# Attention and two MoE layers on one core: each score computed once instead of twice, with its exponential transposed

## The chip, the cores and the metric

The kernel runs on one core of a Trainium2 chip. A core has TensorE (PE in the profile; PEld is its weight load), VectorE (DVE), ScalarE (ACT), GpSimd (POOL) and SyncE (SP), which issues most of the DMAs. Each takes its instructions in order, and they meet through semaphores. SBUF holds 128 partitions by columns; TensorE writes to PSUM, here 8 banks of 128 x 512 fp32. The metric is the device time of one execution in microseconds (us).

## The reference

```python
# attention: q, k, v are (2, 8, 1152, 64)
q_pool = q.reshape(B, H, S // 2, 2, D).mean(axis=3)
scores = scale * np.matmul(q_pool, k.transpose(0, 1, 3, 2))
scores = scores - np.max(scores, axis=-1, keepdims=True)
attn = np.exp(scores)
attn = attn / (np.sum(attn, axis=-1, keepdims=True) + 1e-09)
out = np.matmul(attn, v)
x = out.transpose(0, 2, 1, 3).reshape(1152, 512)
# MoE 1: (1152 x 512) @ (512 x 2048), a rational function of h, @ (2048 x 512)
# MoE 2: the same shapes, with softplus between the products
```

Two queries are averaged into one, so each of the 16 heads has 576 query rows against 1152 keys of 64 columns.

## The kernel before, in words

Heads are taken in pairs: 8 pairs, then MoE 1, then MoE 2. Every fp32 operand of a product is split into a rounded part and the remainder (`fp32r`, names ending in h and l, or hi and lo), and a product is built from two or three passes of such parts. A pair's queries and keys are loaded, transposed on TensorE (`tr_k`, `tr_q`), split by ScalarE (the rounded part) and VectorE (the remainder), and brought by SBUF-to-SBUF DMAs into `KS`, `QQ` and `QL` (`ksXy`, `qqXy` and `qlXy`: X is the pair's parity, y the head).

The attention computes each score twice. `p1_fill` (L431) computes it with queries on partitions, 128 rows by 384 keys, only for the row maximum, which VectorE takes (`p1_max`, L437). There are 27 such units in a pair: 9 row tiles of 128 queries over both heads, times 3 blocks of keys. The maxima are transposed and written as extra rows beside the query remainder (`shift_a`, `shift_t`, `shift_m`). `s_step` (L482, L483) computes the score again with keys on partitions, 128 x 288, and these extra rows subtract the maximum within the product. ScalarE takes the exponential (L489) and rounds two of them together to `ph` (L500); GpSimd subtracts to `pl`; `pv` multiplies in three passes (L516 to L518), the denominator as 64 columns of -1 beside V. In the last pair PV is one pass over unrounded exponentials (L514). `xev_a` and `xev_b` normalise and split the result into `xh` and `xl`.

The order is written by step numbers: a pair has 36 steps, `at(t, fn)` puts work at a step, and a scheduler then orders the engines. The maxima of pair j+1 are taken in the steps of pair j. The weights of the MoE layers come as 64-bit words and are converted on the chip: `w_abs` (ScalarE), two passes of `w_conv` (VectorE), then `w_split` (ScalarE, then VectorE). Sixteen weight tiles are prepared during the attention, three of them spread over the middle pairs and thirteen at steps of four from step 15 of pair 6 on. The MoE stages stand in program order behind it. The VectorE subtractions are all in a helper, so they have its line (L126).

Of the kernel before, what the change touches and what calls it, by code (L numbers as in the profile page):

```python
# [19 lines left out]
    wu=1,  # L20
    ft=2,
    lv=0,
    pv=15,
    pvd=8,
    pe=8,
    ped=3,
    pq=8,
    tk=12,
    tkd=3,
    tke=1,  # L30
    tq=21,
    tqd=3,
    tqe=0,
    ks0=21,
    q0=27,
    ks1=35,
    q1=45,
    kh0=-17,
    kh1=2,
    p1o=-2,  # L40
    p1m=1,
    s0=23,
    s1=40,
    st0=8,
    st1=8,
    sm=0,
    sg=1,
    po=7,
    ps=9,
    xa=16,  # L50
    xb=19,
    w0=-12,
    wd=3,
    wc=14,
    wg=4,
    wh=1,
    ce=10,
    ph=1,
    xl=1,
    vl=1,  # L60
# [23 lines left out]
)


def attn_moe_kernel(tc, q, k, v, w1_in, w1_out, moe_a, moe_b, w2_in, w2_out, out):
# [21 lines left out]
    def at(t, fn, pr=0):
        ev.append((t, pr, len(ev), fn))  # L110

    def behind(fn, *engines):
        with ExitStack() as es:
            for e in engines:
                es.enter_context(tc.issue_after(st["last", e]))
            fn()

    def high(fn, *a):
        with tc.high_priority():
            fn(*a)  # L120
# [858 lines left out]
```

## Time and profile before

| | |
|---|---|
| median of 3 runs (lowest, highest) | 743.1 us (742.61, 743.12) |
| profiled execution: span | 740.7 us |
| its granted TensorE clock, mean | 0.993 |
| busy: PE, DVE, ACT, POOL | 719.3, 543.4, 491.0, 228.9 us |
| score for the maximum, first | 9.2 us |
| first MoE product | 325.28 us |
| DMA | 70.76 MB, mean 96 GB/s |

The profiled execution gives its span, from the first to the last instruction, and no other time of its own; the timed runs lie 2.4 us above it. A matmul row's time is from its start to the end of its drain, so rows of consecutive matmuls overlap; the chain of waits gives the time from one to the next. Rows of ScalarE and VectorE overlap a little too.

### The profile page before, as it was taken

The numbers are of one execution on the slowest core, as the hardware profiler recorded it, in microseconds if no ns is written. First come the engines' busy times: TensorE is split into PE (matmuls) and PEld (weight loads), VectorE is DVE, ScalarE is ACT, GpSimd is POOL, SyncE is SP. The second block draws the span as 40 slices with busy tenths as digits, with TensorE's granted clock in tenths as the row PEclk, the third lists the DMA queues.
The fourth block names the chain that finished last, engine by engine and source line by source line (L and its number), as shares of the span: only waits on it lengthen the run. The fifth ranks groups of instructions, "written<-read, shape, count | busy, mean of one in ns | idle before, by whom it ended". The sixth has DMA issues, their size and how long they took to land.

```text
span 740.7 us, 11685 instructions
## 1 busy us (share of the span) xinstructions
PE 719.3 (97%) x4216; PEld 677.0 (91%) x4216; DVE 543.4 (73%) x938; ACT 491.0 (66%) x945; POOL 228.9 (31%) x197
## 2 busy tenths in 40 slices
PE   8999999999999997997999999999999999999998
PEld 5699999999999997887999999999898999999896
DVE  6877778787877679779999999999786676621122
ACT  3278888888888887877778777876465464422221
POOL 5278787878787776020000000000000000000000
PEclk9999999999999999998999999999999999999999
DMA  5776574747453434542221121210023333201011
GB/s 138 165 183 139 125 180 96 179 98 179 99 122 71 95 86 124 178 151 66 71 58 58 58 85 58 87 58 29 28 86 119 109 114 114 86 1 42 1 43 42
DMA packets 64841, 70.76 MB, mean 96 GB/s; under 512 B 24632, under 2 KB 53136, under 8 KB 64784
## 3 DMA queue, kind: packets, MB, share of 16 engines
q1 hardware_dynamic: 63600, 69.04, 35.1%
q10 hardware_dynamic: 1184, 0.98, 0.4%
q8 instruction: 33, 0.54, 0.3%
q14 instruction: 24, 0.20, 0.1%
HBM read 47.71 MB, written 2.36 MB: 68 GB/s over the span
## 4 chain that ended last, share of the span: by engine, by line
PE 81%; DVE 10%; ACT 4%; issue 3%; DMA 1%; POOL 0%; DVEq 0%; ACTq 0%; SPq 0%
PE acc L769 14%; PE h L747 13%; PE p L431 10%; PE h L666 9%; PE acc L715 9%; PE s L482 5%; PE s L483 5%; PE pv L518 4%; PE pv L516 4%; PE pv L517 4%; PE pv L514 3%; PE wm L269 1%; DMA wraw<-in_moe_w_in_dram 1%; DVE p L689 1%; DVE m L691 1%
## 5 line engine op out<-in xcount | busy, mean ns | idle before, releaser
L126 POOL TENSOR_TENSOR pl<-p,ph 128x576 fp32r<-128x576 f32 x126 | 180.9, 1447 | 53.5 <-ACT ph L500 40.8
L437 DVE TENSOR_REDUCE nm<-p 128x1 f32<-128x384 f32 x216 | 116.2, 553 | 47.8 <-PE p L431 45.6
L489 ACT ACTIVATE p<-s 128x288 f32<-128x288 f32 x252 | 100.8, 407 | 28.2 <-PE s L483 26.7
L126 DVE TENSOR_TENSOR gl<-p,gh 128x384 fp32r<-128x384 f32 (+1 forms) x72 | 49.6, 689 | 90.7 <-ACT gh L756 89.8
L666 PE MATMUL h<-xh,w 128*128 128x384 f32 x384 | 100.7, 342 | 4.4 <-DVE p L690 4.4
L747 PE MATMUL h<-xh,w 128*128 128x384 f32 x384 | 98.1, 336 | 0.1
L755 ACT ACTIVATE p<-h 128x384 f32<-128x384 f32 x48 | 23.6, 491 | 108.4 <-PE h L747 108.4
L715 PE MATMUL acc<-gh,w 128*128 128x384 f32 x384 | 92.9, 337 | 1.3 <-ACT gh L676 1.2
L769 PE MATMUL acc<-w,gh 128*128 128x512 f32 x288 | 90.1, 394 | 0.0
L500 ACT CAST ph<-p 128x576 fp32r<-128x576 f32 x126 | 84.6, 671 | 2.3
L518 PE MATMUL pv<-pl,v 128*128 128x288 f32 x252 | 74.8, 297 | 1.1 <-POOL pl L126 1.1
L666 PEld LDWEIGHTS h<-xh,w 128*128 128x128 f32 x384 | 71.2, 192 | 4.8 <-issue 4.7
L516 PE MATMUL pv<-ph,v 128*128 128x288 f32 x252 | 75.2, 299 | 0.0
L517 PE MATMUL pv<-ph,v 128*64 128x288 f32 x252 | 74.3, 295 | 0.0
L747 PEld LDWEIGHTS h<-xh,w 128*128 128x128 f32 x384 | 70.1, 188 | 4.2 <-ACT p L755 0.4
L715 PEld LDWEIGHTS acc<-gh,w 128*128 128x128 f32 x384 | 68.6, 188 | 2.8 <-ACT gh L676 2.8
L666 PE MATMUL h<-xl,w 128*128 128x384 f32 x192 | 65.4, 341 | 0.0
L747 PE MATMUL h<-xl,w 128*128 128x384 f32 x192 | 64.6, 337 | 0.0
L769 PEld LDWEIGHTS acc<-w,gh 128*128 128x128 f32 x288 | 53.5, 188 | 9.0
L715 PE MATMUL acc<-gl,w 128*128 128x384 f32 x192 | 59.3, 337 | 0.3 <-DVE gl L126 0.3
L769 PE MATMUL acc<-w,gl 128*128 128x512 f32 x144 | 56.9, 395 | 0.0
L518 PEld LDWEIGHTS pv<-pl,v 128*128 128x128 f32 x252 | 47.5, 188 | 1.9 <-POOL pl L126 1.6
(167 smaller groups left out, 1638.7 us busy)
## 6 DMA issues: line engine op xcount, KB each, us to landing
wraw<-in_moe_w_in_dram SPq DMA_DIRECT2D x32, 512.0 KB, 4.0
wraw<-in_moe_w_out_dram SPq DMA_DIRECT2D x32, 512.0 KB, 3.3
kr<-in_k_dram SPq DMA_DIRECT2D x15, 288.0 KB, 3.8
vr<-in_v_dram SPq DMA_DIRECT2D x7, 576.0 KB, 3.7
qr<-in_q_dram SPq DMA_DIRECT2D x15, 256.0 KB, 4.3
out_dram<-m SPq DMA_DIRECT2D x15, 128.0 KB, 1.8
kha<-ks0a SPq DMA_DIRECT2D x4, 288.0 KB, 3.0
khb<-ks0b SPq DMA_DIRECT2D x4, 288.0 KB
```

What stands on the lines that cost most here:

```text
L126: return eng.tensor_tensor(out=o, in0=a, in1=b, op=ALU.subtract)
L431: m = nc.tensor.matmul(out=o, lhsT=l, rhs=r, start=(a == 0), stop=(a == len(mm) - 1))
L437: nc.vector.tensor_reduce(out=st["nm", j][:, t, e:e + 1], in_=st.pop(("p1", j, u)), axis=AX.X, op=ALU.max, negate=True)
L489: st["last", "exp"] = nc.scalar.activation(out=st["p"][:, s % 2], in_=t, func=AF.Exp).ins
L500: nc.scalar.copy(out=ph, in_=p)
L516: nc.tensor.matmul(out=st["pv", j, g], lhsT=h, rhs=ph, start=(c == 0), stop=False)
L517: nc.tensor.matmul(out=st["pv", j, g][0:64], lhsT=l, rhs=ph, start=False, stop=False)
L518: nc.tensor.matmul(out=st["pv", j, g], lhsT=h, rhs=pl, start=False, stop=(c == C - 1))
L666: nc.tensor.matmul(out=h, lhsT=w[:, wi, wd], rhs=x[:, d, xcols(c)], start=(n == 0), stop=(n == 3 * ND - 1))
L715: nc.tensor.matmul(out=st["acc", c, d], lhsT=w[:, wi, wd], rhs=g, start=(first and n == 0), stop=(last and n == 2))
L747: nc.tensor.matmul(out=h, lhsT=w[:, wi, d * 128:(d + 1) * 128], rhs=x[:, d, xcols(c)], start=(n == 0), stop=(n == len(mm) - 1))
L769: nc.tensor.matmul(out=st["acc", c, t], lhsT=g[:, t * 128:(t + 1) * 128], rhs=w[:, wi], start=(first and n == 0), stop=(last and n == 2))
```

## The change

Each score is computed once, with queries on partitions, in the 128 x 384 units that before served only the maximum (`score`, L459). The three units of a row tile stay in PSUM (four buffers, pool `pS`) until VectorE has taken their maxima (L466) and the smallest of the three negated maxima (L470); ScalarE then takes the exponential in place of the second score, with that column as its bias, and has the instruction add up its row as well (L479). TensorE transposes the exponential in three 128 x 128 pieces (`spread`, L430). For two units of three ScalarE rounds the transposed tile to `ph` and VectorE subtracts to `pl`; for the third ScalarE copies it to SBUF (`c`), and GpSimd rounds and subtracts. PV takes two passes (L559): `ph` times V's both parts side by side, 128 columns, and `pl` times the rounded part. GpSimd adds the three row sums, VectorE takes the reciprocal, TensorE transposes it (64 rows), and VectorE multiplies. In all pairs, the last too, this is done alike. The copies of the keys to `KH` and the extra rows go.

The order is no longer by steps and a scheduler. Every operation gets a time: the number of its row tile (9 in a pair) plus an offset from the tables `O`, `OT` and `OJ`. `run` sorts each engine by these and emits them so. The thirteen weight tiles are put 0.8 row tiles apart, from just ahead of the last pair. One line of a table stands here for the three.

```diff
-    pp1 = sb(name="pp1", bufs=3, space=PSUM)
-    pps = sb(name="pps", bufs=3, space=PSUM)
-    ppv = sb(name="ppv", bufs=2, space=PSUM)
+    pS = sb(name="pS", bufs=4, space=PSUM)
+    pT = sb(name="pT", bufs=3, space=PSUM)
+    pA = sb(name="pA", bufs=1, space=PSUM)
...
-        nc.tensor.matmul(out=t, lhsT=KS[i][x][:, ks], rhs=QQ[i][x][:, cs], start=True, stop=False)
-        nc.tensor.matmul(out=t, lhsT=KH[x][:, ks], rhs=QL[i][x][:, cs], start=False, stop=True)
...
-        st["last", "exp"] = nc.scalar.activation(out=st["p"][:, s % 2], in_=t, func=AF.Exp).ins
...
-        nc.scalar.copy(out=ph, in_=p)
-        sub(nc.gpsimd, pl, p, ph)
...
-        nc.tensor.matmul(out=st["pv", j, g], lhsT=h, rhs=ph, start=(c == 0), stop=False)
-        nc.tensor.matmul(out=st["pv", j, g][0:64], lhsT=l, rhs=ph, start=False, stop=False)
-        nc.tensor.matmul(out=st["pv", j, g], lhsT=h, rhs=pl, start=False, stop=(c == C - 1))
...
+        b = st["t"]
+        when = b + O.get(kind, 0)
+        if kind in OT:
...
+    def run():
+        need = [set(o[3]) for o in ops]
...
+        queue = {}
+        for i in sorted(range(len(ops)), key=lambda i: (ops[i][0], i)):
+            queue.setdefault(ops[i][1], []).append(i)
+        done = [False] * len(ops)
+        with tc.manual_schedule():
+            while any(queue.values()):
+                heads = [q[0] for q in queue.values() if q and all(done[d] for d in need[q[0]])]
+                i = min(heads, key=lambda i: (ops[i][0], i))
+                queue[ops[i][1]].pop(0)
+                done[i] = True
+                ops[i][2]()
...
+MODES = "ABA"
+NS, NT_, NP_, NPH, NCP = 4, 3, 6, 5, 2
...
+        op("S" + str(e), "PE", fn=fn, R=R, W=[k], new=[("s", NS)], **mm(173 * (3 if diag else 2 * len(srcs))))
...
+        op("M" + str(n % 3), "DVE", fn=lambda: nc.vector.tensor_reduce(
+            out=NM[i][:, n:n + 1], in_=tl[k], axis=AX.X, op=ALU.max, negate=True),
+           R=[k], W=[("NM", i, n)], **dve(384))
+        if n % 3 == 2:
+            op("B", "DVE", fn=lambda: nc.vector.tensor_reduce(
+                out=MB[i][:, t:t + 1], in_=NM[i][:, 3 * t:3 * t + 3], axis=AX.X, op=ALU.min),
+               R=[("NM", i, 3 * t + e) for e in G3], W=[("MB", i, t)], **dve(3))
...
+            o = tl[p] = late.tile([128, 384], F32, tag="p", name="p", bufs=NP_)
+            nc.scalar.activation(out=o, in_=tl[k], func=AF.Exp, bias=MB[i][:, t:t + 1], accum_out=DEN[i][:, n:n + 1])
...
+        op("T" + str(e), "PE", fn=lambda: transpose(k, [(tl[p][:, a * 128:(a + 1) * 128], 128) for a in G3]),
+           R=[p], W=[k], new=[("t", NT_)], **mm(327))
...
+        if md == "A":
+            for m, (s0, w, o, h, l) in enumerate(d):
+                    act_copy(view(h, o, w), src(k, s0, w))
+                op("L" + str(e), "DVE", fn=lambda s0=s0, w=w, o=o, h=h, l=l: sub(
+                    nc.vector, view(l, o, w), src(k, s0, w), view(h, o, w)), R=[k, h], W=[l], **dve(3 * w))
...
+        def fn():
+            tl[c] = late.tile([128, 384], F32, tag="c", name="c", bufs=NCP)
+            (nc.scalar.copy if md == "B" else nc.vector.tensor_copy)(out=tl[c], in_=tl[k][:, 0:384])
...
+                nc.gpsimd.tensor_copy(out=view(h, o, w), in_=src(c, s0, w))
...
+            op("L" + str(e), "POOL", fn=lambda s0=s0, w=w, o=o, h=h, l=l: sub(
+                nc.gpsimd, view(l, o, w), src(c, s0, w), view(h, o, w)), R=[c, h], W=[l], **pool(3 * w))
...
+                mm_ = [(acc, v2[:, c], tl[h]), (acc[0:64], v2[:, c, 0:64], tl[l])]
+                for a, (o, p, r) in enumerate(mm_ if c < C - 1 else mm_[::-1]):
+                    nc.tensor.matmul(out=o, lhsT=p, rhs=r[:, m, 0:w], start=(c == a == 0), stop=(c == C - 1 and a == 1))
...
+            nc.gpsimd.tensor_add(out=r, in0=d[:, :, 0], in1=d[:, :, 1])
+            nc.gpsimd.tensor_add(out=r, in0=r, in1=d[:, :, 2])
+            nc.gpsimd.tensor_scalar(out=r, in0=r, scalar1=1e-9, scalar2=None, op0=ALU.add)
...
+        op("D1", "DVE", fn=lambda: nc.vector.reciprocal(out=r, in_=r), R=W, W=W, **dve(24))
...
+            rt, [(RC[i][:, t:t + 1].to_broadcast([128, 64]), 128) for t in GT[g]], 64),
...
+            nc.scalar.copy(out=tl[u][:, 0:w], in_=tl[k][64:128, 0:w])
...
+        op("U1", "DVE", fn=lambda: nc.vector.tensor_add(out=tl[u][:, 0:w], in0=tl[k][0:64, 0:w], in1=tl[u][:, 0:w]),
...
+            nc.vector.tensor_mul(out=tl[xs][64 * x:64 * x + 64, c0:c0 + w], in0=tl[rt][0:64, o0:o0 + w],
+                                 in1=tl[u][:, 0:w])
...
+        for h, key in enumerate((st["khi", j], st["klo", j])):
+            op(f"dk{x}", fn=lambda h=h, key=key: fdma(KS[i][x][64 * h:64 * h + 64], tl[key][r]),
+               R=[(*key, g) for g in G3], W=[("KS", i, x, h, g) for g in G3], **spq(lat=4500))
...
+        op("wl", fn=lambda: w_load(i), W=[raw], new=[("raw", 2)], **spq(lat=4000))
+        op("w0", "ACT", fn=lambda: w_abs(i), R=[raw], W=[pk], new=[("pk", 3)], **act(512))
+        op("w1", "DVE", fn=lambda: w_conv(i, 0), R=[pk], W=[pk], port=True, ns=340, lat=150)
+        op("w2", "DVE", fn=lambda: w_conv(i, 2), R=[raw, pk], W=[pk], port=True, **dve(512))
+
...
+        op("w3", "ACT", fn=fh, R=[pk] + pool_[1], W=[w], **act(512))
+        op("w4", "DVE", fn=fl, R=[pk, w], W=[w], port=True, **dve(512))
...
+        for n in range(NRA + NRB - 1):
+            a = n < NRA
+            at(te + T["ce"] + T["prea"] + n * T["pred"], weight, NE + n,
+               ((lambda: st["wra"]) if a else (lambda: st["wrb"]), [("wra",) if a else ("wrb",)]))
...
+    "S0": -1.2121,
...
```

TensorE in the middle of a pair, before (`p1` is a score for the maximum, `s` the second score, `pv` the result):

```order
L482 MATMUL s_2894<-qq0a_101,ks0a_95 128x288
L483 MATMUL s_2894<-ql0a_105,kha_99 128x288
L431 MATMUL p1_2907<-ks1a_97,qq1a_103 128x384
L431 MATMUL p1_2907<-ks1a_97,ql1a_107 128x384
L516 MATMUL pv_2879<-ph_2839,v20_111 128x288
L517 MATMUL pv_2879<-ph_2839,v20_111 64x288
L518 MATMUL pv_2879<-pl_2840,v20_111 128x288
```

A round of one score for the maximum, one PV step and one second score repeats.

The same engine now, about row tile 6 of a pair (`s` the score, `t` a transposed tile, `p` an exponential, `pv` the result):

```order
L459 MATMUL s_3979<-ks0b_101,qq0b_105 128x384
L459 MATMUL s_3979<-ks0b_101,ql0b_109 128x384
L430 MATMUL t_3982<-ident_58,p_3977 128x128 x3
L459 MATMUL s_3988<-ks0b_101,qq0b_105 128x384
L459 MATMUL s_3988<-ks0b_101,ql0b_109 128x384
L430 MATMUL t_3991<-ident_58,p_3986 128x128 x3
L430 MATMUL t_4005<-ident_58,p_3995 128x128 x3
L459 MATMUL s_4009<-ks0b_101,qq0b_105 128x384
L459 MATMUL s_4009<-ks0b_101,ql0b_109 128x384
L559 MATMUL pv_4015<-ph_3872,v20_114 128x320
L559 MATMUL pv_4015<-pl_3873,v20_114 64x320
```

Between two scores stand transposes of exponentials and pieces of PV; a score needs a buffer that an exponential of an earlier row tile has given up.

VectorE in the last pair, before (`pk` and `w` are a weight being converted, `xm`, `pv` and `xs` the normalising):

```order
L528 SCALAR_TENSOR_TENSOR xm_4802<-pv_4717,xr_4801 64x288
L186 TENSOR_SCALAR pk_4808<-pk_4808 128x512
L529 TENSOR_TENSOR pv_4717<-pv_4717,xr_4801 64x288
L192 SCALAR_TENSOR_TENSOR pk_4808<-wraw_4769,pk_4808 128x512
L532 SCALAR_TENSOR_TENSOR xs0_4653<-xm_4802,pv_4717 64x288
L126 TENSOR_TENSOR w_4817<-pk_4771,w_4817 128x512
L126 TENSOR_TENSOR w_4840<-pk_4808,w_4840 128x512
L186 TENSOR_SCALAR pk_4877<-pk_4877 128x512
```

Only weights and the normalising are left there, since the maxima of this pair were taken in the pair before.

VectorE in the last pair now (`nm` a maximum, `mb` the smallest of three, `pl` a remainder, `u` and `xs` the normalising):

```order
L313 TENSOR_TENSOR pl_4331<-t_4304,ph_4330 128x3x128
L377 SCALAR_TENSOR_TENSOR pk_4328<-wraw_4258,pk_4328 128x512
L313 TENSOR_TENSOR pl_4357<-t_4335,ph_4356 128x3x128
L466 TENSOR_REDUCE nm1_61<-s_4353 128x1
L466 TENSOR_REDUCE nm1_61<-s_4383 128x1
L466 TENSOR_REDUCE nm1_61<-s_4376 128x1
L313 TENSOR_TENSOR pl_4331<-t_4379,ph_4330 128x3x128
L470 TENSOR_REDUCE mb1_65<-nm1_61 128x1
L371 TENSOR_SCALAR pk_4395<-pk_4395 128x512
L377 SCALAR_TENSOR_TENSOR pk_4395<-wraw_4313,pk_4395 128x512
L592 TENSOR_TENSOR u_4406<-pv_4319,u_4406 64x256
L313 TENSOR_TENSOR pl_4357<-t_4412,ph_4356 128x3x128
```

The conversion of the weights now stands among the maxima, with the maxima queued behind it.

## Rows read from the trace of the kernel before

**Rows 1.** Page: the span, and the chain that ended last, by engine.

```profile
span 740.7 us, 11685 instructions
...
PE 81%; DVE 10%; ACT 4%; issue 3%; DMA 1%; POOL 0%; DVEq 0%; ACTq 0%; SPq 0%
```

**Rows 2.** Windows: one middle pair, and the last pair; busy us by engine.

```profile
133.00:170.00 37.00, 36.36 (x255) 35.71 (x254) 28.91 (x58) 32.46 (x74) 30.62 (x25) 1.00 0.59 138
293.00:332.00 39.00, 35.81 (x186) 30.95 (x185) 30.73 (x56) 28.91 (x68) 6.86 (x9) 0.96 0.55 165
```

**Rows 3.** Chain of waits, middle of a pair: start, us, TensorE line, count.

```profile
150.97 0.35 PE p L431 x2
...
151.33 0.13 PE pv L516
...
155.78 0.33 PE tk L350 x3
```

**Rows 4.** Milestones: V rows two pairs apart (chain), first score (tile), first MoE product (timeline).

```profile
117.01 1.58 DVE v L126
...
191.03 1.58 DVE v L126
...
L431 PE MATMUL p<-ks0a,qq0a x51: 335/340/446, 9.2 to 234.1; 128*128 128x384 f32 x51
...
325.28 0.72 PE L666 MATMUL h<-xh,w 128*128 128x384 f32 x2
```

**Rows 5.** ScalarE, groups by shape, and one timeline row of two exponentials.

```profile
L489 ACT ACTIVATE p<-s 128x288 f32<-128x288 f32 x252 | 100.8, 407 | 28.2 <-PE s L483 26.7
...
L356 ACT CAST khi<-tk 128x384 fp32r<-128x384 f32 x21 | 9.8, 468 | 9.3 <-PE tk L350 8.1 <-DVE nm L437 1.1
...
L526 ACT ACTIVATE xr<-pv,eps 64x288 f32<-64x288 f32 x32 | 15.9, 498 | 2.6 <-PE pv L518 1.7 <-PE pv L514 0.2
...
L259 ACT ACTIVATE b_sb<-b_sb 128x2 f32<-128x2 f32 x1 | 0.2, 202 | 0.0
...
153.92 0.70 ACT L489 ACTIVATE p<-s 128x288 f32<-128x288 f32 x2
```

**Rows 6.** VectorE: a subtraction by shape; timeline of two maxima and one weight.

```profile
L126 DVE TENSOR_TENSOR klo<-tk,khi 128x384 fp32r<-128x384 f32 x21 | 11.7, 556 | 2.2 <-ACT khi L356 1.8
...
156.12 1.02 DVE L437 TENSOR_REDUCE nm<-p 128x1 f32<-128x384 f32 x2
...
304.01 0.43 DVE L186 TENSOR_SCALAR pk<-pk 128x512 int32<-128x512 int32 x1
...
304.47 0.69 DVE L192 SCALAR_TENSOR_TENSOR pk<-wraw,pk 128x512 int32<-128x512 int32 x1
...
305.08 0.68 DVE L126 TENSOR_TENSOR w<-pk,w 128x512 fp32r<-128x512 f32 x1
```

**Rows 7.** GpSimd, groups by shape: subtraction, query sums, two kinds of copies.

```profile
L126 POOL TENSOR_TENSOR pl<-p,ph 128x576 fp32r<-128x576 f32 x126 | 180.9, 1447 | 53.5 <-ACT ph L500 40.8 <-PE pv L518 4.1 <-PE s L483 3.5
...
L339 POOL TENSOR_TENSOR qs<-qr 128x256 f32<-128x256 f32 x14 | 10.6, 773 | 10.0 <-PE tq L375 6.4 <-DMA qr<-in_q_dram 3.7
...
L540 POOL CAST xh<-xs 128x288 fp32r<-128x288 f32 x2 | 1.9, 941 | 22.1 <-DVE xs L532 22.1
...
L297 POOL CAST qq0a<-qq0a 64x512 fp32r<-64x512 f32 x1 | 0.6, 604 | 1.6 <-ACT qq0a L291 1.6
```

**Rows 8.** VectorE lines: a short reduction and a short copy, ns min/median/max.

```profile
L445 DVE TENSOR_REDUCE m<-nm x16: 151/157/173, 27.8 to 291.1; 128x5 f32<-128x15 f32 x16
...
L446 DVE CAST s<-m x16: 159/267/1874, 29.0 to 292.9; 128x5 fp32r<-128x5 f32 x16
```

**Rows 9.** TensorE timeline after its longest wait in the attention.

```profile
296.76 1.30 PE L514 MATMUL pv<-ph,p 128*128 128x288 f32 x2 [3.19 <-issue]
...
298.34 0.44 PE L516 MATMUL pv<-ph,v 128*128 128x288 f32 x1
```

**Rows 10.** DMA issues: a key copy between SBUF tiles, us to landing.

```profile
ks1a<-klo SPq DMA_DIRECT2D x4, 288.0 KB, 4.7
```

More of the change, by code (lines that the diff above doesn't have):

```diff
@@ L19 @@
     warm=24,
[L20 to L60, printed above, removed]
+    xp=1,
+    vp=1,
+    fq=-5,
+    f1=0.62,
+    fd=0.3,
+    v0=-4.2,
+    one=4,
+    ce=-1.5,
+    cv=2.5,
+    pre0=6,
+    prea=0.3,
+    pred=0.8,
     l1=2,
@@ L100, in attn_moe_kernel @@
     NCH = NT // TOK
-    ST = 4 * C
+    ST = 27
     NE, NRA, NRB = T["ne"], 7, 7
     LAG1, LAG2 = T["l1"], T["l2"]
-    ev = []
     st = {}
[L109 to L120, printed above, removed]
+    ops, wrote, read, rings = [], {}, {}, {}
@@ new lines, in attn_moe_kernel, with act, dve, pool @@
+    G3 = range(3)
+    def act(n, extra=0):
+        return dict(ns=n * 0.917 + 50 + extra, lat=150)
+    def dve(n):
+        return dict(ns=n / 0.96 + 70, lat=150)
+    def pool(n, two=True):
+        return dict(ns=n * (2.36 if two else 1.1) + 90, lat=80, port=True)
+    def mm(n):
+        return dict(ns=n, lat=240)
+    def spq(eng="SP", ns=450, lat=3500):
+        return dict(eng=eng, ns=ns, lat=lat)
+    def act_copy(out, in_):
+        nc.scalar.copy(out=out, in_=in_)
+    def transpose(k, srcs, rows=128, w=128):
+        o = tl[k] = pT.tile([128, 512], F32, tag="t", name="t")
+        for i, (a, n) in enumerate(srcs):
+            nc.tensor.transpose(o[0:rows, i * 128:i * 128 + n], a, ident[0:n, 0:n])
@@ L264, in warm @@
-    def warm(n):
-        if "wm" not in st:
-            st["wm"] = ppv.tile([128, 512], F32, tag="wm", name="wm")
-        t = st["wm"]
-        for _ in range(n):
-            nc.tensor.matmul(out=t[0:64, 0:256], lhsT=zero[:, 0:64], rhs=zero, start=True, stop=True)
-    def first_k(x, g):
-        kr = st["kr", 0]
-        t = pps.tile([128, 512], F32, tag="s", name="tk")[0:64, 0:384]
-        for i in range(3):
-            nc.tensor.transpose(t[:, i * 128:(i + 1) * 128], kr[:, x, 3 * g + i], ident)
-        s = slice(384 * g, 384 * (g + 1))
-        st["last", "act"] = nc.scalar.copy(out=KS[0][x][0:64, s], in_=t).ins
-        st["last", "dve"] = sub(nc.vector, KS[0][x][64:128, s], t, KS[0][x][0:64, s]).ins
@@ L797, in attn_moe_kernel @@
     if True:
[L798 to L815 removed]
+        attention()
+        run()
+        pA.release()
+        pT.release()
+        pS.release()
         late.release()
@@ L918, in attn_moe_kernel @@
                 if every(n, T["r2"]):
-                    behind(w_step, "gh")
+                    with tc.issue_after(st["last", "gh"]):
+                        w_step()
             m = n - 2 * LAG2
```

987 lines of the change are left out of this document (585 added, 402 removed), and 35 rows, old and new, of the table OT.

## The prediction

> **What bounds the kernel now.** I read the page first. The chain that ended last is TensorE for 81% of a span of 740.7 us, so what is worth something is what TensorE waits for or is spared [rows 1]. Next the windows: in a middle pair TensorE is busy for 36.36 of 37.00 us, ScalarE for 32.46, GpSimd for 30.62, VectorE for 28.91, at a granted clock of 1.00 [rows 2]. The attention is TensorE's work from end to end, with the others close behind. The milestones divide the span: the first score starts at 9.2 us, MoE 1 at 325.28, and between two V rows that are two pairs apart lie 74.02 us, so a pair takes 37.0 [rows 4]. MoE's code is unchanged and begins in both kernels with sixteen weights prepared or nearly so; its first 384 tokens need only pairs 0 to 3. So I take the 415.4 us from 325.28 to the end as they are and ask only when MoE 1 begins. The timed runs are 2.4 us above the span, and I carry that over.
>
> **TensorE per pair.** The chain gives the time from one matmul to the next: 0.35 us for two of 384 columns, about 0.135 for one of 288, 0.33 for three transposes [rows 3]. Before: 57 score matmuls for the maxima (24 units by two, the three of the mixed row tile by three) x 0.175 = 10.0; 72 of the second score and 108 of PV x 0.135 = 24.3; 14 transposes x 0.11 = 1.5. That is 35.8, and 1.2 us of waiting make the 37.0.
> The change takes away the 72 second scores (9.7) and one PV pass of three (4.9). It adds 81 transposes of exponentials (8.9) and 10 of reciprocals (1.1). After: scores 10.0, PV in two passes 72 x 0.135 = 9.7, transposes 105 x 0.11 = 11.6: 31.2 us. So TensorE is spared 4.6 us a pair.
>
> **The others per pair.** ScalarE: an exponential of 288 columns takes 407 ns alone and two take 0.70 us, so about 0.11 overlaps; a copy of 384 out of PSUM takes 468, hence 0.36 from start to start; a column as bias adds 91 (498 against 407, same columns) [rows 5]. No row shows the row sum taken with an exponential: its lower bound is nothing, its upper one the smallest ScalarE instruction, 202 ns [rows 5]. The two are near, and I take 0.10. 27 exponentials x 0.55 = 14.9, 27 copies x 0.36 = 9.7, four copies of the accumulator x 0.3 and five of keys and queries together 2.8: 27.4 us, or 24.7 to 30.1.
> VectorE: two maxima take 1.02 us, one 0.55, hence 0.47 a maximum and, at the like 556 ns, a subtraction [rows 6]. 27 maxima 12.7, 18 remainders 8.5, nine short reductions x 0.16 = 1.4 [rows 8], eight operations on the accumulator 3.0, keys and queries 2.2, reciprocals 0.6: 28.4 us.
> GpSimd: a subtraction of 576 columns takes 1447 ns, hence 0.96 for 384 [rows 7]. Its rounding copy has two prices: 604 ns for 512 columns, or 0.5 for 384, and 941 for 288, or 1.25. I take the former, the nearer in width, and keep the latter for the range. Nine copies 4.5 and nine subtractions 8.7, query sums 2.0, V 4.3, the output split 2.2, row sums 1.2: 22.9, or 34.4 by the dear copy. So per pair nothing is above TensorE's 31.2 but GpSimd in its bad case.
>
> **What is late next.** Before, an exponential passed from TensorE to ScalarE, to GpSimd, and back to TensorE. Now a tile crosses eight times: score, maximum, exponential, transpose, rounding, remainder, PV, normalising, and every engine works to a fixed order. I put TensorE's waits at twice the 1.2 us of before, so 33.5 us a pair; 31.2 with almost none is the lower end.
>
> **The last pair.** VectorE has no keys and queries there (26.2), but thirteen weights: from one row to the next 0.46 and 0.61, and 0.61 for the third at the same overlap [rows 6], 1.68 each, 21.8 in all. Sum 48. Before, the maxima of this pair were behind it when most weights came, and VectorE was busy for only 30.73 of 39.00 us [rows 2]. A copy between SBUF tiles that meets GpSimd takes up to 1874 ns instead of 159, while a reduction of the same size class never leaves 151 to 173 [rows 8]; the 39 weight operations are of the exposed sort. I add 3 us for blocking and take off 2 for weight work that follows the last maximum: 49 us. No blocking gives 46, 0.2 us on each operation 54.
> [...]
>
> **The sum.** First score 9.2 (loads and first transposes are as before); first exponential 2.5 later (three scores 1.05, the last one's drain, maximum, smaller reduction); seven pairs 7 x 33.5 = 234.5; the last pair 49; from its last exponential over transposing to the first MoE product 3, for MoE's first products stand ahead of the last PV group in TensorE's order. 298.2 us against 325.3: MoE begins 27.1 us earlier. 743.1 - 27.1 = 716.0 us. Break-even is a middle pair of 37.4 us.
>
> **Rivals.**
> *Almost no waits.* ScalarE and VectorE have 3 to 4 us to spare per pair and TensorE fills up: 31.6 a pair, 47 for the last. MoE begins at 282.9: 701 us. For it: the order was laid so that independent work stands between dependent steps. Against: eight crossings.
> *Keys late at the turn of a pair.* The keys of the next pair are transposed about two thirds through a pair, then split, then copied by DMA; a copy lands 4.7 us after issue [rows 10], and scores can't begin without it. From the transposes to the next pair's first score TensorE has about 7.3 us of other work, the path needs about 0.25 + 1.0 + 1.2 + 4.7 = 7.2. If it is 1.2 late each time, seven turns cost 8: 724 us. Before, keys were a whole pair ahead.
> *GpSimd bounds.* At 34.4 of work and 2 of hand-off a pair takes 36.4, and MoE begins at 318.5: 736 us. For it: both dear copies of the trace. Against: they ran in the last pair beside VectorE's weight passes, which the middle pairs hardly have.
> *The score buffers (slower).* Three of four PSUM buffers hold one row tile till its maximum is known. The loop: second exponential done, the third score of the next tile runs 0.35 and drains 0.17, maximum 0.55, reduction 0.16, two exponentials 1.2, four hand-offs 0.25: 2.7 us. With one transposed tile and a PV piece ahead on TensorE (0.9), a remainder on VectorE (0.47) and a copy on ScalarE (0.36) it is 4.4 a row tile, 39.6 a pair. The last pair is then 51: MoE begins at 342.9, 761 us. It decides from 37.4 / 9 = 4.15 on. For it: the order shows such work between scores. Against: the average row tile has 31.2 / 9 = 3.5 of TensorE's work, and the offsets spread the interposed pieces over three scores.
> [...]
> [...]
> That the second score doesn't really go is out: the order has no 288-column score left.
>
> **Chances.** The forecast 0.45; almost no waits 0.14; keys late 0.14; GpSimd 0.11; score buffers 0.08; clock 0.08. Less than 0.2% (1.5 us) can't be told from no change here. Only GpSimd's case reaches to that: 0.02 of it. Faster 0.82, same 0.02, slower 0.16. The range from 699 to 740 us takes in the first four cases and leaves out the two slower ones and the far ends.
>
> **What would show it.** Right: a pair of 32 to 35 us between V's or another pair-wise row; no score row of 288 columns, 648 rows of transposed exponentials (81 a pair); MoE's first product between 285 and 315 us and the rest 415 us long; the last pair longer than the others, VectorE over 90% busy there. Wrong: exponentials over 0.7 us, GpSimd copies over 1 us, TensorE waiting for `ks` copies at each turn, waits for ScalarE ahead of every third score, a granted clock under 0.95 in the middle, or a MoE stage that changes its length, which I have put at nothing.

## The result and the profile after

The changed kernel takes 726.1 us (median of 4 runs, 724.6 to 727.1) against 742.9: a ratio of 0.977, 95% interval 0.976 to 0.979. It is 16.8 us faster; 27.1 were forecast, and the time lies in the range but 10.1 us above the number.

The page of the changed kernel: its span, and the chain that ended last by engine. It answers to [rows 1].

```profile
span 722.7 us, 11854 instructions
...
PE 60%; DVE 19%; ACT 12%; issue 4%; DMA 2%; SPq 1%; POOL 0%; DVEq 0%; ACTq 0%
```

TensorE's share of the chain falls from 81% to 60%, and VectorE's rises from 10% to 19%: the chain now changes engine more often. Where it does so is read from milestones. The score products of three pairs, by the key tile that they read (ns of one, min/median/max, then first and last start; the first row is that of the whole span), and below them the first MoE product in TensorE's timeline; they answer to [rows 4]:

```profile
L459 PE MATMUL s<-ks0a,qq0a x51: 338/421/688, 10.3 to 237.0; 128*128 128x384 f32 x51
...
L459 PE MATMUL s<-ks1a,qq1a x12: 337/378/440, 50.2 to 64.8; 128*128 128x384 f32 x12
...
L459 PE MATMUL s<-ks0a,qq0a x12: 338/383/442, 85.3 to 99.0; 128*128 128x384 f32 x12
...
L459 PE MATMUL s<-ks1a,qq1a x12: 331/421/447, 257.4 to 274.0; 128*128 128x384 f32 x12
```

```profile
304.54 0.60 PE L970 MATMUL h<-xh,w 128*128 128x384 f32 x2
```

From first score to first score, pair 0 takes 39.9 us (10.3 to 50.2), pair 1 35.1 (to 85.3), pairs 1 to 6 together 207.2 (50.2 to 257.4, or 34.5 each), and pair 7 47.1 to the first MoE product. The MoE stage begins at 304.5 instead of 325.28, 20.8 us earlier, and 2.8 of these are lost again behind it (418.2 us to the end instead of 415.4). Busy time by engine in pair 2 and in pair 7 (length, PE, PEld, DVE, ACT, POOL, granted clock, DMA share, GB/s), against [rows 2]:

```profile
85.30:119.80 34.50, 33.08 (x235) 29.88 (x235) 30.79 (x77) 31.22 (x96) 24.48 (x44) 1.00 0.54 131
257.40:304.50 47.10, 37.34 (x244) 30.97 (x243) 46.46 (x108) 43.67 (x121) 23.36 (x37) 1.00 0.44 134
```

In a middle pair TensorE is busy for 33.1 of 34.5 us, ScalarE for 31.2, VectorE for 30.8: three engines within 2.3 us of each other. In pair 7 VectorE is busy for 46.5 of 47.1 us and ScalarE, with the same weights, for 43.7. GpSimd stands far behind (24.5 and 23.4 us). All that TensorE waited for in pair 2 (us in total, times, longest):

```profile
PE s L459 <- ACT p L479: 0.8, 2, 0.6
PE t L430 <- ACT c L529: 0.3, 1, 0.3
PE t L430 <- DVE pl L313: 0.2, 1, 0.2
```

No key copy is among TensorE's waits, and no wait ahead of every third score. The chain of waits of pairs 2 and 3 by line (85 to 154 us), and that of pair 7 (257.4 to 304.5 us); both lists go on to the right:

```profile
by line: PE t L430 23.1%; PE s L459 23.0%; PE pv L559 20.0%; ACT p L479 10.6%; ACT ph L425 5.3%; ACT u L589 3.6%; ACT c L529 3.5%; issue 3.0%; DVE pl L313 2.6%; ACT khi L699 2.4%; DVE nm L466 1.6%; ACT w L870 1.4%; DVE mb L470 0.2%; ACTq L5
```

```profile
by line: ACT p L479 16.2%; DVE nm L466 14.1%; issue 9.5%; ACT ph L425 6.9%; DVE pk L377 6.7%; DVE pk L371 5.9%; ACT pk L365 5.9%; PE t L430 5.6%; DVE pl L313 5.3%; DVE w L313 5.2%; PE s L459 4.9%; DVE xs L601 2.6%; ACT w L870 2.5%; PE pv L5
```

In the middle pairs TensorE has 66% of the chain and ScalarE 27%; in pair 7 the listed lines of VectorE sum to 40%, ScalarE's to 32%. ScalarE's timeline in pair 2 shows what the exponential with its sum costs; it answers to [rows 5]:

```profile
103.65 0.48 ACT L529 COPY c<-t 128x384 f32<-128x384 f32 x1
104.03 0.48 ACT L425 CAST ph<-t 128x384 fp32r<-128x384 f32 x1
104.43 0.58 ACT L479 ACTIVATE p<-s,mb 128x384 f32<-128x384 f32 x1
104.91 0.19 ACT L479 ACTIVATION_READ_ACCUMULATOR p<-s,mb 128x1 f32 x1
105.00 0.57 ACT L479 ACTIVATE p<-s,mb 128x384 f32<-128x384 f32 x1
105.46 0.20 ACT L479 ACTIVATION_READ_ACCUMULATOR p<-s,mb 128x1 f32 x1
105.56 0.58 ACT L479 ACTIVATE p<-s,mb 128x384 f32<-128x384 f32 x1
```

The sum is an instruction of its own with 0.2 us on its row. Adding the two durations would give 0.78 us, but they overlap: from start to start it is 0.56 to 0.57. A copy takes 0.48 on its row and 0.38 from start to start.

Where the forecast and the trace part, in us:

| Stretch | forecast | measured | off by |
|---|---|---|---|
| first score | 9.2 | 10.3 | +1.1 |
| pair 0 | 33.5 | 39.9 | +6.4 |
| pairs 1 to 6 | 201.0 | 207.2 | +6.2 |
| pair 7, to the first MoE product | 54.5 | 47.1 | -7.4 |
| MoE stage | 415.4 | 418.2 | +2.8 |
| around the span | 2.4 | 3.4 | +1.0 |

The sum is +10.1 us. The last row is no stage of the kernel: every execution lies 1.9 to 2.1 us above its own span, and the profiled one was the fastest of the four.

### The profile page after: what moved, and what is told of

Same layout as the page of the kernel before. It is cut to its first block, busy times and chain, and to the rows that moved or that the text cites. A ratio compares the mean times of both kernels' runs of the same rounds, so it can differ in the third digit from the quotient of the medians.

```text
span 722.7 us, 11854 instructions
## 1 busy us (share of the span) xinstructions
PE 685.3 (95%) x4076; PEld 629.0 (87%) x4076; DVE 559.4 (77%) x1080; ACT 495.2 (69%) x1135; POOL 205.2 (28%) x357
## 4 chain that ended last, share of the span: by engine, by line
PE 60%; DVE 19%; ACT 12%; issue 4%; DMA 2%; SPq 1%; POOL 0%; DVEq 0%; ACTq 0%
PE acc L1073 14%; PE h L1051 13%; PE s L459 8%; PE t L430 8%; PE pv L559 7%; PE acc L1019 5%; PE h L970 4%; ACT p L479 4%; DVE nm L466 2%; ACT ph L425 2%; DMA wraw<-in_moe_w_in_dram 2%; DVE m L995 2%; DVE p L993 2%; DVE m L1005 2%; DVE pl L313 2%
## 5 line engine op out<-in xcount | busy, mean ns | idle before, releaser
L466 DVE TENSOR_REDUCE nm<-s 128x1 f32<-128x384 f32 x216 | 116.5, 550 | 23.4 <-PE s L459 22.1
L479 ACT ACTIVATE p<-s,mb 128x384 f32<-128x384 f32 x216 | 125.9, 593 | 5.1 <-DVE mb L470 4.6
L430 PE MATMUL t<-ident,p 128*128 128x128 f32 x648 | 99.0, 276 | 8.8 <-ACT p L479 4.2
L1059 ACT ACTIVATE p<-h 128x384 f32<-128x384 f32 x48 | 23.6, 492 | 108.5 <-PE h L1051 108.5
L430 PEld LDWEIGHTS t<-ident,p 128*128 128x128 f32 x648 | 79.0, 142 | 18.2 <-ACT p L479 9.6
L559 PE MATMUL pv<-ph,v 128*128 128x256 f32 (+1 forms) x288 | 89.5, 321 | 1.2 <-DVE u L592 0.6
L313 DVE TENSOR_TENSOR pl<-t,ph 128x384 fp32r<-128x384 f32 (+1 forms) x160 | 80.3, 509 | 7.0 <-ACT ph L425 5.4
L425 ACT CAST ph<-t 128x384 fp32r<-128x384 f32 (+1 forms) x160 | 70.0, 453 | 18.8 <-PE t L430 12.7
L559 PE MATMUL pv<-pl,v 128*64 128x256 f32 (+1 forms) x288 | 77.4, 295 | 1.6 <-POOL pl L313 1.6
L313 POOL TENSOR_TENSOR pl<-c,ph 128x384 fp32r<-128x384 f32 (+1 forms) x80 | 75.0, 941 | 4.6
L539 POOL CAST ph<-c 128x384 fp32r<-128x384 f32 (+1 forms) x80 | 41.3, 520 | 71.6 <-ACT c L529 66.8
```

The costliest lines, as they stand in the source:

```text
L313: return eng.tensor_tensor(out=o, in0=a, in1=b, op=ALU.subtract)
L425: nc.scalar.copy(out=out, in_=in_)
L430: nc.tensor.transpose(o[0:rows, i * 128:i * 128 + n], a, ident[0:n, 0:n])
L466: op("M" + str(n % 3), "DVE", fn=lambda: nc.vector.tensor_reduce(out=NM[i][:, n:n + 1], in_=tl[k], axis=AX.X, op=ALU.max, negate=True), R= ...
L479: nc.scalar.activation(out=o, in_=tl[k], func=AF.Exp, bias=MB[i][:, t:t + 1], accum_out=DEN[i][:, n:n + 1])
L539: nc.gpsimd.tensor_copy(out=view(h, o, w), in_=src(c, s0, w))
```

## The experiments

Each is an edit of the changed kernel. Three theories stood at the start. *TensorE* sets the middle pairs, as forecast. *ScalarE* sets them instead, since a score buffer is held until the sum is read out (in pair 2 the two scores that wait for an exponential start at 105.15 and 108.98 us, each 0.05 us after the end of a sum's row). And *VectorE* alone sets pair 7, with ScalarE's nearly equal busy time as the rival.

### 1. Without the row sums

```diff
-nc.scalar.activation(..., bias=MB[i][:, t:t + 1], accum_out=DEN[i][:, n:n + 1])
+nc.scalar.activation(..., bias=MB[i][:, t:t + 1])     # DEN is set once, on GpSimd
```

> Leaves out the row sums: the exponentials are written without an accumulated sum, and the denominators are set once to a constant. In the changed kernel a middle pair takes 34.5 us, TensorE is busy for 32.0 to 32.7 of 33 to 34 us and waits 1.3 us; ScalarE is busy for 29.2 to 30.7. ScalarE's exponential with its sum takes 0.57 us to the next instruction, a copy of the same size 0.38. Theory TensorE (its work sets the middle pairs): at most its waits go, middle pair 33.2 to 34.4, pair 7 unchanged within 1 us, time 717 to 726. Rival ScalarE (each score buffer is held until the sum is read out): 27 x 0.17 = 4.6 us less in each of eight pairs, middle pair about 30, time 686 to 694.

Measured: 723.2 us (ratio 0.974, 0.972 to 0.975). Pair 2:

```profile
87.00:121.50 34.50, 33.20 (x237) 29.97 (x236) 31.01 (x78) 29.23 (x69) 24.71 (x44) 1.00 0.57 132
```

ScalarE is spared 2.0 us and the pair is as long as it was, where the rival wanted 4.6 us less. ScalarE doesn't set it. The 2.9 us that the run gains lie elsewhere: pairs 1 to 6 together take 204.5 us instead of 207.2 (1.4 of this in pair 1) and the MoE stage 416.7 instead of 418.2, while pair 0 is 3.0 longer, at a granted clock of 0.74 instead of 0.83 from 10 to 30 us. Without the sum, exponentials follow each other after 0.46 to 0.47 us, so the sum costs 0.10, as the prediction had taken it; the 0.17 of this expectation came from comparing with a copy, and was wrong.

### 2. Without the low pass of PV

```diff
-for a, (o, p, r) in enumerate(mm_ if c < C - 1 else mm_[::-1]):   # high, low
+for o, p, r in mm_[:1]:                                            # high alone
```

> Leaves out the second pass of PV, the one with the low parts of the exponentials (36 products a pair, about 0.117 us apart, 4.2 us); the low parts are still made. Theory TensorE: a middle pair goes from 34.5 to 30.9 to 32, where ScalarE (busy 30 to 31) takes over; seven pairs give 18 to 25 us, pair 7, which VectorE bounds, gives nothing; time 701 to 708. Rival ScalarE: middle pair 34 to 34.5, time 723 to 726.

Measured: 712.3 us (0.960, 0.958 to 0.962). Neither theory gave this. Pair 2:

```profile
83.90:117.10 33.20, 30.94 (x200) 25.27 (x199) 30.32 (x77) 31.29 (x95) 24.76 (x43) 1.00 0.59 139
```

TensorE lost 36 products, 4.8 us by the prediction's 0.135, and the middle pair only 1.3. ScalarE is busy for 31.3 of 33.2 us there, and in the chain of waits from 84 to 150 us its exponentials alone have 24.5%, TensorE's products and transposes together 17%, where they had 66% before this edit:

```profile
by line: ACT p L479 24.5%; ACT ph L425 9.3%; PE s L459 8.2%; ACT c L529 7.4%; issue 6.6%; PE t L430 6.4%; DMA vr<-in_v_dram 6.2%; DVE nm L466 6.2%; DVE pl L313 4.4%; ACT u L589 4.2%; ACT khi L699 3.7%; PE pv L559 2.1%; SPq L638 2.0%; SPq L6
```

So TensorE set the pair, but ScalarE stands 1.3 us behind it. Pairs 1 to 6 together are 9.8 us shorter, 1.6 each.

### 3 to 5. The thirteen weights of the last pair

Run 3 leaves out VectorE's part of them, run 4 ScalarE's, run 5 both. What is left out is replaced by fills on GpSimd:

```diff
 # run 3
-w_conv(i, 0)
-w_conv(i, 2)
-sub(nc.vector, w[:, 1], g, w[:, 0])
+nc.gpsimd.memset(w[:, 1], 0.0)
 # run 4
-w_abs(i)
+nc.gpsimd.memset(st["pk", i], 0.0)
-nc.scalar.copy(out=w[:, 0], in_=g)
+nc.gpsimd.memset(w[:, 0], 0.02)
 # run 5: both
```

> Leaves out VectorE's part of the thirteen weights that are converted in the last pair (two bit steps and the low part, 13 x 1.78 = 23 us; GpSimd clears the low part in its place). Theory VectorE bounds the last pair (99% busy there): pair 7 goes from 47.1 to the 34 to 36 of the others, time 713 to 716. Rival ScalarE bounds it just as much (it is busy 46 of 47 us there, 16 of them with the same weights): pair 7 stays at 44 to 47, time 722 to 726.

> Leaves out ScalarE's part of the same thirteen weights (the magnitude and the high part, 13 x 1.25 = 16 us; GpSimd sets both tiles instead). Theory VectorE alone bounds the last pair: pair 7 stays at 45 to 47 us, time 724 to 727. Rival ScalarE: pair 7 goes to 35 to 40, time 714 to 720. If both bound it equally, neither this kernel nor the one without VectorE's part gains more than 3 us.

> Leaves out both parts of the thirteen weights of the last pair, VectorE's (23 us) and ScalarE's (16 us); GpSimd sets the tiles. Without VectorE's part alone pair 7 went from 47.1 to 44.1 us with ScalarE busy for 43.3 of them. Theory two engines (ScalarE's work stands right behind VectorE's): pair 7 falls to 34 to 37 us, the length that TensorE sets elsewhere, and the first gate tile of the MoE stage comes 20.5 to 21.5 us after the stage's first product, as in the kernel before, instead of 23.5; time 712 to 716. Rival (the transfers of the weights, or the end of a pair itself, hold the last pair): pair 7 stays at 40 to 44, time 718 to 721.

Measured: run 3 719.5 us (0.969, 0.967 to 0.970), run 4 727.5 (0.980, 0.978 to 0.981), run 5 719.2 (0.969, 0.967 to 0.970); pair 7 takes 44.1, 51.2 and 41.8 us. Pair 7 of run 3, then of run 5:

```profile
257.00:301.10 44.10, 36.67 (x248) 31.47 (x246) 29.24 (x73) 43.33 (x121) 23.89 (x48) 1.00 0.48 152
```

```profile
257.40:299.20 41.80, 37.08 (x246) 32.78 (x245) 29.29 (x74) 32.95 (x99) 32.89 (x68) 0.96 0.58 174
```

With 17 us of work off VectorE, ScalarE is busy for 43.3 of 44.1 us: two engines bound pair 7, not VectorE alone. The time of run 3 lies below the rival's 722 to 726 because its MoE stage is 415.3 us long again. Run 4 is longer than the changed kernel, which no theory said. The first bit step of a weight, ns min/median/max, in pair 7 of the changed kernel and of run 4:

```profile
L371 DVE TENSOR_SCALAR pk<-pk x13: 407/415/960, 257.3 to 304.3; 128x512 int32<-128x512 int32 x13
```

```profile
L371 DVE TENSOR_SCALAR pk<-pk x12: 407/418/2033, 256.7 to 305.4; 128x512 int32<-128x512 int32 x12
```

The median stays and a single one grows to 2033 ns (in the chain of waits 1.96 us, from 270.1 on). GpSimd fills 22 tiles in this pair, 12.3 us of work, and its subtractions grow from 1063 to 1207 ns on average; that its work held up this one isn't shown. In sum VectorE is busy for 47.9 us instead of 46.5, and TensorE's granted clock falls too, to 0.90 over pair 7. Which of these makes up the 4.1 us wasn't parted. Run 5 is spoilt by its fills as well: they stand in the chain of waits of pair 7. So runs 4 and 5 say nothing on ScalarE's part by itself, and run 9 was made.

### 6. Without the row sums and the low pass

```diff
 # the edits of runs 1 and 2 together
-accum_out=DEN[i][:, n:n + 1]
-(acc[0:64], v2[:, c, 0:64], tl[l])
```

> Leaves out the row sums and the low pass of PV together. Alone they took 0.1 and 1.3 us off a middle pair; without the low pass ScalarE was busy for 31.3 of 33.2 us. Theory of near-equal engines (TensorE 33, ScalarE 31, VectorE 30 us of work a pair, the longest sets it with 1.5 to 2 us of waits): VectorE is what is left, middle pair 31.5 to 32.5, time 704 to 709. Rival (the hand-offs between the engines set 33 us whatever their work): middle pair stays at 33.0 to 33.3, time 711 to 713.

Measured: 709.0 us (0.955, 0.953 to 0.956). Pair 2:

```profile
84.20:116.30 32.10, 29.88 (x199) 25.45 (x199) 29.99 (x77) 28.99 (x68) 24.74 (x44) 1.00 0.62 144
```

The pair goes on to 32.1 us. In this pair the sums were worth nothing in run 1 and are worth 1.1 us here, where TensorE no longer stands in front; over pairs 1 to 6 it is 2.7 us there and 5.9 here. A fixed hand-off of 33 us is out.

### 7. More transposes

```diff
 transpose(k, [(tl[p][:, a * 128:(a + 1) * 128], 128) for a in G3])
+if e == 1:
+    for a in G3:
+        nc.tensor.transpose(tl[k][:, a * 128:(a + 1) * 128], tl[p][:, a * 128:(a + 1) * 128], ident)
```

> Transposes every third tile of exponentials twice, the same result written over itself: 27 more transposes a pair, 0.11 us apart, 3.0 us of TensorE's time. Theory TensorE sets the middle pairs: nearly all of it is seen, middle pair 36.8 to 37.6, seven pairs 16 to 21 us, pair 7 at most 1 more; time 743 to 748. Rival (ScalarE or the hand-offs set them, TensorE has slack): middle pair 34.6 to 35.6, time 727 to 734.

Measured: 742.1 us (1.000, 0.999 to 1.001). Pair 2:

```profile
88.20:125.60 37.40, 35.99 (x264) 33.04 (x263) 31.50 (x77) 31.72 (x96) 24.89 (x44) 1.00 0.52 123
```

It grows by 2.9 us for 3.0 of added work, at a clock of 1.00; over pairs 1 to 6 it is 15.1 for 17.8. The added transposes also hold up what follows the tile, but TensorE's listed waits in the pair don't grow with it (1.2 us, against 1.3). Added work on TensorE counts nearly in full, removed work only up to the next engine: that is what an engine in front of two near-equal ones looks like.

### 8. The start filled

```diff
+at(T["fq"] - 0.001, warm, 6)
+at(-0.4, warm, 6)
 at(T["fq"], first_q, 0, 1)
```

> Puts six of the warming products into each of two idle stretches of TensorE at the start (from 8.7 and 11.9 us). In the changed kernel the granted clock is 0.50 to 0.65 from 12 to 19.5 us, after TensorE had been busy for 0.5 of 2 us and had waited 1.4; the kernel before shows 1.00 there. Theory clock: it stays at 1.00 and pair 0 goes from 39.9 to 36 to 37.5 us, time 722 to 724. Rival (pair 0 is long because of what it prepares: the second head, the next pair's keys and queries, each behind loads): pair 0 stays at 39 to 40, time 725 to 727.

Measured: 722.8 us (0.973, 0.972 to 0.975), faster than the changed kernel (0.976 to 0.979). Windows of 2 us of the changed kernel, then of this one (the figure behind the five engines is the granted clock):

```profile
8.00:10.00 2.00, 0.52 (x3) 0.25 (x3) 1.87 (x5) 0.60 (x2) 0.13 (x1) 1.00 0.00 0
10.00:12.00 2.00, 1.82 (x9) 1.47 (x9) 1.27 (x5) 0.22 (x1) 1.24 (x3) 1.00 0.00 0
12.00:14.00 2.00, 0.59 (x2) 0.53 (x3) 1.42 (x4) 1.31 (x5) 0.27 (x1) 0.65 0.00 0
14.00:16.00 2.00, 2.00 (x10) 1.90 (x9) 1.27 (x3) 0.75 (x3) 0.00 (x0) 0.50 0.00 0
16.00:18.00 2.00, 2.00 (x10) 1.78 (x9) 0.90 (x2) 1.64 (x5) 1.00 (x2) 0.50 0.00 0
```

```profile
12.00:14.00 2.00, 1.36 (x9) 0.82 (x8) 1.44 (x5) 1.29 (x5) 0.30 (x1) 1.00 0.00 0
14.00:16.00 2.00, 2.00 (x15) 1.70 (x15) 1.76 (x4) 1.52 (x5) 0.08 (x1) 1.00 0.00 0
16.00:18.00 2.00, 1.35 (x10) 1.01 (x11) 1.74 (x5) 2.00 (x7) 1.85 (x3) 1.00 0.00 0
```

TensorE stays at a granted clock of 1.00 from 12 to 18 us, where it had 0.50 to 0.65, and does 15 products and transposes instead of 10 from 14 to 16 us. But pair 0 goes only from 39.9 to 38.3 us, short of the 36 to 37.5: the clock is part of it, and the smaller part. A single pair 0 is a loose measure: in runs 3, 4, 5 and 9, which don't change it, it takes 39.6 to 41.1 us, and with the filled start (runs 10 and 11) 38.0 and 38.4. By the medians the filled start is worth 3.3 us: the four executions of the changed kernel have mean granted clocks of 0.992 to 0.995 and take 724.6 to 727.1 us, those of run 8 have 0.999 to 1.000 and take 722.5 to 723.1.

### 9. No conversion in the last pair

```diff
+if i >= NE:    # one DMA of the same size from an earlier weight's tile, no engine's work
+    fdma(w, st["w", order[i % NE]]); return
```

> Leaves out the conversion of the thirteen weights of the last pair on every engine: each tile is copied by one DMA of the same size from an earlier weight's tile. In the run without both engines' parts GpSimd's fills of the tiles (13 x 3 x 0.47 = 18 us) stood in the chain of waits of pair 7, and GpSimd was busy for 31 of its last 42 us; this run has none. Theory two engines (VectorE and ScalarE, both with these weights, bound pair 7): pair 7 goes from 47.1 to 34 to 37.5 us, time 712 to 716. Rival (the transfers, or the end of a pair itself): pair 7 stays at 40 to 43, time 718 to 721. On the MoE stage: if VectorE's backlog delays its first gate tile (23.5 us after the first product, 20.5 in the kernel before), it comes after 20 to 21.5 us here; else after 23 to 24.

Measured: 717.0 us (0.965, 0.963 to 0.967). Pair 7:

```profile
259.40:298.80 39.40, 35.75 (x248) 31.51 (x246) 30.48 (x76) 33.21 (x100) 19.51 (x37) 1.00 0.50 188
```

39.4 us lies between the two expectations. Its last score group starts at 293.2, so 33.8 us are as in a middle pair, and 5.6 are the pair's own end (last exponential, transposes, PV), which in other pairs lies beside the next one's scores. So the weights cost pair 7 7.7 us: 3.0 of these went with VectorE's part in run 3, and 4.7 more when ScalarE's went too. This run also has no loads of these weights and none of run 3's fills, so the 4.7 isn't shown to be ScalarE's alone.

### 10 and 11. Two versions meant to be faster

```diff
 # both: the filled start of run 8, and one weight more in the middle pairs
-NS, NT_, NP_, NPH, NCP = 4, 3, 6, 5, 2
+NS, NT_, NP_, NPH, NCP = 4, 3, 5, 5, 2
-NE, NRA, NRB = 3, 7, 7
+NE, NRA, NRB = 4, 7, 6
 # 11 alone, for every other weight of the last pair
-sub(nc.vector, w[:, 1], g, w[:, 0])
+sub(nc.gpsimd, w[:, 1], g, w[:, 0])
```

> A version meant to be faster: the filled start (723 us by itself), and one weight more converted in the middle pairs, four there and twelve in the last pair, for which the exponentials get five buffers instead of six. TensorE bounds the middle pairs, so ScalarE's 1.25 and VectorE's 1.78 us should be free there: pair 7 goes from 47.1 to 45 to 46 us, the others stay at 34.5, time 720 to 722. Rival (five buffers hold up ScalarE, or the weight lengthens its pair): a middle pair grows by 0.5 us or more, time 723 to 727.

> The version before, and every other weight of the last pair has its low part subtracted on GpSimd instead of VectorE (6 x 0.68 us off VectorE, which was busy for 99% of pair 7). Theory two engines: ScalarE is busy for 46 of 47 us there with work that does not move, so pair 7 gains at most 1 us, time 720 to 722. Rival VectorE alone: pair 7 is 3 to 4 us shorter, time 717 to 719. Rival contention (VectorE's operations on the weights took 0.55 and 0.78 us instead of 0.46 and 0.69 where GpSimd filled the tiles): pair 7 no shorter or longer, time 722 to 725.

Measured: 723.0 us (0.974, 0.972 to 0.975) and 724.4 (0.976, 0.974 to 0.977). Run 10 gains nothing over run 8, and pair 7 is 47.0 us long. The line of the second bit step shows why for that part: it runs twelve times within pair 7 in the changed kernel and in run 10 alike, so the weight taken away was not in it.

```profile
L377 DVE SCALAR_TENSOR_TENSOR pk<-wraw,pk x12: 671/688/990, 259.2 to 302.0; 128x512 int32<-128x512 int32 x12
```

```profile
L377 DVE SCALAR_TENSOR_TENSOR pk<-wraw,pk x12: 671/686/989, 257.4 to 300.1; 128x512 int32<-128x512 int32 x12
```

In run 11 pair 7 takes 49.9 us instead of 47.0, although VectorE has five subtractions less: its first bit step now takes up to 1507 ns and its second up to 1265. The two lines, and a window in the middle of pair 7 (columns as above):

```profile
L371 DVE TENSOR_SCALAR pk<-pk x13: 401/420/1507, 256.4 to 306.3; 128x512 int32<-128x512 int32 x13
L377 DVE SCALAR_TENSOR_TENSOR pk<-wraw,pk x12: 671/682/1265, 258.3 to 303.6; 128x512 int32<-128x512 int32 x12
```

```profile
285.00:295.00 10.00, 9.17 (x42) 8.27 (x43) 8.23 (x22) 7.08 (x19) 5.28 (x9) 0.66 0.45 157
```

GpSimd's subtraction of a weight takes 1370 ns on average. VectorE's bit steps grow by 3.1 us in sum (14.5 to 17.6), as much as its subtractions fell (7.6 to 4.5). So VectorE won nothing. What made the pair longer still stands in the window: TensorE at a granted clock of 0.66, and VectorE idle for 1.8 of 10 us behind it. What lowered the clock there wasn't tried. That GpSimd held up the long bit steps of this run isn't shown either. In pair 7 of the changed kernel the two longest, 960 and 990 ns, stand beside its operations for 0.7 and 1.0 us (a subtraction from 256.92 us on; a rounding and a sum from 262.67 on); but others stand beside them for 0.4 and 0.6 us and don't grow (0.41 us at 289.89, 0.69 at 301.96).

### 12. Constants moved out of pair 0

```diff
-at(3.5, moe_consts)
+at(12.5, moe_consts)        # beside the filled start
```

> The filled start again, and the constants of MoE 1 (three small VectorE operations and one of ScalarE's, 0.43 to 0.15 us, with their load) moved from row tile 4 of pair 0 to row tile 4 of pair 1. In pair 0 they stand in the chain of waits at 31.7 to 32.3 us, ahead of the smaller reduction that ScalarE's exponentials wait for, in the stretch from 30 to 39 us where TensorE is busy for only 7.2 of 10. If this queueing on VectorE is part of what makes pair 0 long, pair 0 goes from 38.3 to 37 to 37.8 us and the time to 721.5 to 722.5. Rival (the stretch is full anyway with the second pair's keys and queries): pair 0 stays at 38 to 38.6, time 722.5 to 723.3.

Measured: 733.1 us (0.988, 0.986 to 0.990). Pair 0 goes to 37.6 us, as expected, from 38.0 to 38.4 in the three other runs with the filled start. But pair 1 goes from 34.9 to 45.3. Its chain of waits:

```profile
68.88 0.59 SPq L433
69.52 0.59 SPq L433
70.15 0.59 SPq L433
70.79 0.60 SPq L433
71.44 0.59 SPq L847
72.07 3.33 DMA b_sb<-in_moe_b_dram
75.43 0.21 ACT b_sb L851
```

The constants' load moved with them, and in SyncE's queue it now stands behind the copies of the next pair's queries, of which the first could go only at 67.1 us, when the scores of pair 1 had read the tile that it overwrites. ScalarE waited 7.8 us for 8 bytes a partition, and TensorE had no work from 70 to 75 us. When it had, at 77.1 us, its granted clock was 0.50 (0.73 from 80 to 86 us), which is part of the 10.4 us.

## Why the prediction was right in kind and 10 us off

**TensorE sets the middle pairs: shown.** Its work was put at 31.2 us a pair and the waits at 2.3. Run 7 shows that its work counts, run 1 that ScalarE's hardly does. The waits are 34.5 - 31.2 = 3.3 us, and TensorE is idle for 1.4 of them; the rest would be waits that a busy TensorE hides, since a product's row is 0.34 us long where 0.175 lie between two. That is not shown. Doubling the 1.2 us of before was too little: the term "waits" is mis-sized by 1.0 us a pair, 6.2 us over six pairs.

**The other engines.** ScalarE was put at 27.4 us and is busy for 31.2 in pair 2, VectorE at 28.4 and 30.8. Of this the one weight that is converted in pair 2 is 1.3 and 1.8 us, which the sum doesn't have; in pair 1, without a weight, the two are busy for 29.8 and 28.8, so VectorE's sum was right. The exponential is right (0.55 for 0.57) and so is the sum (0.10). The overlaps of [rows 5, 6] hold where instructions follow each other without a gap (a copy with a row of 0.48 us takes 0.38 from start to start, above); ahead of a wait the whole row counts as busy (in pair 2 ScalarE rounds for 0.48 us from 98.92 on and then waits for 0.68). The price of GpSimd's copy is the cheap one (553 ns for 384 columns on average), and its rival is out. That rival's 34.4 us was not worked out: nine copies at 1.25 instead of 0.5 add 6.8 us to the 22.9, not 11.5.

**Pair 0: the step that failed most (+6.4 us).** The sum took seven equal pairs. Pair 0 also makes the second head's keys and queries, and the next pair's within 7 us (their remainders on VectorE stand at 36.5 to 42.9 us, in pair 2 at 95.0 to 113.2). Of the 6.4 us run 8 gives back 1.6 (the clock) and run 12 another 0.7 (constants ahead of a reduction). What the other 4 are wasn't taken apart; from 30 to 40 us TensorE is busy for 7.2 of 10 and waits for exponentials. In all of pair 0 its listed waits are 4.8 us, against 1.3 in pair 2.

**Pair 7 (-7.4 us).** Right: VectorE is busy for 99% of it, 46.5 us, where 26.2 + 21.8 = 48 were forecast. Wrong: 3 us for blocking, of which the long bit steps (960 and 990 ns) are about 1; and 2.5 + 3 us at its ends, in which VectorE has weights to convert anyway. Part of the 7.4 is only moved: 2.8 us of VectorE's work on the thirteen weights stand behind the first MoE product, up to 309.2 us. Also missed: ScalarE stands just behind.

**The MoE stage (+2.8 us), put at nothing.** From its first product to its first gate tile it takes 23.5 us (304.5 to 328.0) instead of 20.5, and the rest is as long as before (394.7 us for 394.9). Between its parts of the first two gate tiles ScalarE takes the first step of two weights (L365), and of one in run 2, where the first gate tile comes after 21.2 us. ScalarE in the changed kernel, then in run 2 (L986 begins the second gate tile):

```profile
315.70 0.67 ACT L365 ACTIVATE pk<-wraw 128x512 f32<-128x512 f32 x1 [0.18 <-DMA wraw<-in_moe_w_in_dram]
...
318.48 0.68 ACT L365 ACTIVATE pk<-wraw 128x512 f32<-128x512 f32 x1 [1.60 <-DMA wraw<-in_moe_w_in_dram]
319.06 0.98 ACT L986 ACTIVATE p<-h,a_sb 128x768 f32<-128x768 f32 x1
```

```profile
307.72 0.67 ACT L365 ACTIVATE pk<-wraw 128x512 f32<-128x512 f32 x1 [0.32 <-DMA wraw<-in_moe_w_in_dram]
308.29 0.98 ACT L986 ACTIVATE p<-h,a_sb 128x768 f32<-128x768 f32 x1
```

For the second of the two it waits 1.6 us, since that weight's load could go out only when VectorE's second bit step had read its buffer. The chain of waits of the changed kernel:

```profile
313.54 0.92 DVE pk L377
...
314.51 3.88 DMA wraw<-in_moe_w_in_dram
```

So VectorE's backlog of weights comes back by way of a load. The other runs fit: the first gate tile comes after 21.2 us in runs 2, 3, 6 and 9, in which VectorE has 5.8 to 7.2 us of weight operations between the first product and that tile (the kernel before: 6.9), and after 22.7 to 23.6 in all others, which have 7.5 to 10.1. Run 5 is one of these: VectorE has no weight in its pair 7, but 10.1 us of work on the next ones behind the first product. No run moves that load or that step alone, so this is read from traces and not tried.

**The range.** That 726.1 lies within it owes something to chance: pair 0, the middle pairs, the MoE stage and the two small rows are 17.5 us over the forecast, and pair 7, forecast too long, takes 7.4 off again.

**The rivals.** *Almost no waits*, *keys late* and *GpSimd* are refuted by the middle pair and its list of waits; *score buffers* likewise (0.8 us in two waits, where 4.4 us a row tile were needed). *Clock*, 0.08 of the chances, is seen only at the start: over pair 0 the granted clock is 0.91, in pairs 1 to 7 it is 1.00. With 105 transposes a pair, among other products, it is 1.00, and so it is with the 27 more of run 7. Three transposes take 0.33 us at a granted clock of 1.00 (run 12, 62.6 us) and 0.64 at 0.50 (78.2 us).

## What to carry to other kernels

When a change takes work off the engine in front, look first at how far behind the next one stands: here 4.8 us less on TensorE gave 1.3 in pair 2. Sum the first and the last iteration of a pipelined loop by themselves, since the first carries preparation and, here, a stretch at a granted clock of 0.50 to 0.65 (12 to 20 us), and the last an end that nothing lies beside. And when a step is moved, follow its load through the queue that issues it: a few bytes behind seven copies, of which the first had to wait, cost 10 us.
